# Loads of the second pass's h and of wo's pages moved from SyncE's queue to ScalarE's

## The chip, the cores and the metric

The kernel runs on one core of one Trainium2 chip. A core has TensorE (PE, with its weight loads shown as PEld), VectorE (DVE), ScalarE (ACT), GpSimd (POOL) and SyncE (SP), each with its own stream of instructions that it works through in order, and they meet through semaphores. SyncE computes nothing here: its stream holds the DMAs that it issues. The time is device microseconds of one execution; for the kernel before, the median of three runs is 2241.88 us (2241.23 to 2243.62).

## The reference

One transformer block with adaptive layer norm, for one sequence of 2048 tokens by 1024 channels, 32 heads of 32 channels, all in float32:

```python
mod = (silu(c) @ w_mod)            # sa, ca, ga, sb, cb, gb
h = layernorm(x) * (1 + ca) + sa
x = x + ga * A(h)                  # attention
h = layernorm(x) * (1 + cb) + sb
x = x + gb * B(h)                  # token-mixing MLP, 2048 -> 3584 -> 2048 over tokens
# A: q, k, v = h @ wq, h @ wk, h @ wv; the tokens fall into 4 segments s of 512
logits = q_s k_s^T * scale + mask        # -1e9 where key index < query index
a_dot = softmax(logits) @ v_s
a_mem = phi(q_s) M / (phi(q_s) z + 1e-6) # phi(t) = t + 1 for t > 0, else exp(t)
o = sigmoid(beta) * a_mem + (1 - sigmoid(beta)) * a_dot
M, z = M + phi(k_s)^T v_s, z + sum(phi(k_s))   # then o @ wo at the end
```

## The kernel before, in words

**Precision.** Large products run on pairs of reduced-precision parts: an operand is held as a rounded part and the rest, and a product is three matmuls (high by high, high by low, low by high). `split` (L119) makes the two parts, the first on ScalarE, the second on VectorE.

**Attention.** The heads are in eight groups of four (`NG`), the tokens in four segments. One iteration t works on one group and one segment. The 32 iterations are ordered in two passes, `its` (L322): pass one goes through the groups with segments 0 and 1, pass two through the groups again with segments 2 and 3. The normed, transposed input h of a segment is eight pages of 128 x 2 x 512 (one for every 128 channels), in `hpages`. The pool of pages has 16 buffers, which is two segments; so pass two's sixteen pages take over the buffers of pass one's. h of segments 2 and 3 is computed during pass one by `token_tile` (L230) and parked in device memory in `hT1`; `reload_h` (L317) fetches one page, 512 KB. At the end of pass two the same 16 buffers are taken over by the pages of wo, `wop`, which were prepared in `wos` by `wo_split` (L597); a page again is 512 KB.

An iteration has these steps. `project` (L338) multiplies the pages by the group's weights: `nps` (L196) gives k and v, `qps` (L204) gives q. ScalarE and VectorE copy the results out of PSUM; the split q and k are `sg`. `stack` (L328) copies `sg` within the chip by DMA into the layout `sk` (three DMAs for a head, L334 to L336). `maxima` (L431) multiplies q and k (tiles `sx`, `sy`, `sz`, L441), takes maxima on VectorE (L443) and sends them, transposed and negated (`nt`, L451), as two more rows into `sk` by four small DMAs for two heads (L456). `scores` (L470) then multiplies again with these rows (`a`, L477 to L484), and ScalarE takes the exponentials (L478, L481, L485), which leave the two PSUM buffers of the tag `s2` that three products of a head go through in turn. `values` (L494) multiplies by v (`pv`, L506), and the group's output goes out as `ot` to `oT` (L524).

**What sets the order.** The main loop (L632) runs over head steps n, four to an iteration, and in each emits scores of n, maxima of n + 3, values of n - 1 and the projection of n + 8. Weights of the next group are fetched ahead (`load_w`, `wv` and `wq` from `wsp`, L171), rows of w_mod during these steps (`rawm`, L531). Where the code emits an instruction does not fix its place: the program is built with

```python
with tile.TileContext(nc, schedule_with_timeline_sim=True) as tc, ExitStack() as ctx:
```

so a planner lays out each engine's stream when the program is built, by the work that it reckons ready and by the code's order among that. In the kernel before all DMAs are issued by SyncE.

**Around the change.** The loads of h's pages are emitted at steps m = n + 8 = 59 to 66, two to a step, the first eight for segment 2 and the others for segment 3. They need the buffer of the old page free, so they wait for the last `qps` product of pass one that reads it: iteration 14 for the first eight, iteration 15 for the rest. The loads of wo's pages are emitted at steps 123 to 130, again two to a step, sixteen pages of which thirteen are loaded here (the other three in `product`, L727, after the loads of x). They wait likewise for `qps` of iterations 30 and 31. After the attention, `product` (L715) multiplies the output by wo (`po`, L734), the second norm is taken, and the token MLP runs as matrix products with seven multiplications in place of eight (`mix`, L849) until the end.

Of the kernel before, what the change touches and what calls it, by code (L numbers as in the profile page):

```python
# [7 lines left out]
F32 = mybir.dt.float32  # L8
# [37 lines left out]
def attention_and_mlp(ctx, tc, x, wq, wkv, wo, beta, w1, b1, w2, b2, c, wm_a, wm_b, out):  # L46
    nc = tc.nc
    V, A, G, T, SY = nc.vector, nc.scalar, nc.gpsimd, nc.tensor, nc.sync
# [9 lines left out]
    wos = dram.tile([NK, 2, P, 2, 512], F32, name="wos")  # L58
    wsp = dram.tile([NG, 6, P, 2, 512], F32, name="wsp")
    hT1 = dram.tile([2, NK, P, 2, L], F32, name="hT1")  # L60
# [84 lines left out]
    def new_page(name):  # L145
        return page.tile([P, 2, 512], F32R, tag="page", bufs=16, name=name)
# [32 lines left out]
    def load_w(g, pr):  # L179
        res = W[pr, g] = {}  # L180
        for kind, part in (("v", 0), ("v", 1), ("q", 0)):
            load_part(g, pr, kind, part, res)
        if pr == 0:
            keep_w(g)
# [93 lines left out]
    for ct in range(NK):  # L278
        for part in range(2):
# [4 lines left out]
            elif ct >= NSC:  # L284
                for i in range(2):
                    c = slice(512 * i, 512 * i + 512)
# [29 lines left out]

    def reload_h(seg, ct):  # L317
        pg = new_page(f"h{seg}_{ct}")
        SY.dma_start(pg.bitcast(F32), hT1[seg - 2, ct])
        hpages[seg, ct] = pg  # L320

    its = [(pr, g, 2 * pr + i) for pr in range(2) for g in range(NG) for i in range(2)]  # L322
# [138 lines left out]
    @contextmanager  # L461
    def behind(n, engines):

        with ExitStack() as s:
            for e in engines:
                if (n, e) in marks:
                    s.enter_context(tc.issue_after(marks[n, e].ins))
            yield
# [86 lines left out]
    def at(f, n):  # L555
        if 0 <= n < 4 * NI:
            f(n // 4, n % 4)
# [31 lines left out]
    wop = {}  # L589
# [42 lines left out]
    for n in range(-LEADS, 4 * NI + VL):  # L632
        at(scores, n)
        at(maxima, n + LEADS)
        at(values, n - VL)
        m = n + LEADP
        if 0 <= m + 4 < 4 * NI:
            t = (m + 4) // 4
            if its[t][:2] not in W:
                with tc.issue_after(last_sk[0, 3].ins):  # L640
                    load_w(its[t][1], its[t][0])
        if m >= 8:
            at(project, m)
        if 59 <= m < 67:
            seg, ct = 2 + (m - 59) // 4, 2 * ((m - 59) % 4)
            reload_h(seg, ct)
            reload_h(seg, ct + 1)
        if 4 * NI - 5 <= m < 4 * NI + 3:
            i = m - 4 * NI + 5
            for c in (2 * (i % 4), 2 * (i % 4) + 1):  # L650
                wop[c, i // 4] = new_page(f"wo{c}_{i // 4}")
                if c < 5 or i < 4:
                    SY.dma_start(wop[c, i // 4].bitcast(F32), wos[c, i // 4])
        for f, engines in todo.pop(n, ()):
            with behind(n, engines):
                f()
# [428 lines left out]
```

## Time and profile before

| what | value |
|---|---|
| median of three runs | 2241.88 us |
| the profiled execution's own time | 2241.52 us |
| its span, first to last instruction | 2239.8 us |
| mean granted TensorE clock | 0.995 |
| DVE busy | 1672.5 us (75%) |
| ACT busy | 1147.5 us (51%) |
| POOL busy | 748.9 us (33%) |
| loads of h's pages | 469.4 to 508.3 us (issue) |
| loads of wo's pages at L653 | 934.6 to 967.9 us (issue) |

The execution that was profiled took 1.7 us more than its span, and 0.36 us less than the median. Times inside the profile are microseconds from the span's start. "PE sx L441 <- DMA sk<-nt: 5.7, 1, 5.7" in the view of waits reads: TensorE, before instructions of line 441 that write tile sx, stood idle 5.7 us in all, once, at most 5.7 us, and what ended it was the landing of a DMA from nt into sk. SPq is SyncE's stream; a DMA's row there is its issue, not its transfer. A row of a timeline is: start, duration, engine, line, operation, tiles (out<-in), how many were merged, and in brackets the idle time ahead of it with what ended it. Rows of stretches give the busy time of PE, PEld, DVE, ACT and POOL, then the granted clock, the share that the 16 DMA engines were busy, and GB/s.

### The profile page before, as it was taken

How to read it: one execution, taken by the hardware profiler on the slowest of the kernel's cores; microseconds unless marked ns; L12 is line 12 of the kernel's file. 1: busy time of each engine (PE TensorE's matmuls, PEld its weight loads, DVE VectorE, ACT ScalarE, POOL GpSimd, SP SyncE). 2: the span in 40 equal slices, each digit the busy share in tenths (PEclk: the TensorE clock that was granted, in tenths of full speed). 3: DMA queues.
4: the chain of work that ended last, by engine and by line, in shares of the span. 5: the costliest groups of instructions: out<-in, count | busy, mean ns of one | idle time of the engine just before them, and what ended most of it. 6: DMA issues, size and time to landing. Idle time of an engine off the chain costs nothing.

```text
span 2239.8 us, 38394 instructions
## 1 busy us (share of the span) xinstructions
PE 2192.1 (98%) x13802; PEld 1897.4 (85%) x13802; DVE 1672.5 (75%) x3778; ACT 1147.5 (51%) x2106; POOL 748.9 (33%) x847
## 2 busy tenths in 40 slices
PE   7999999998999999999999999999999999999999
PEld 6889898888989999988888888888888888888887
DVE  6687677866777777655758866888888897868687
ACT  6487777765656666655546633533334242424232
POOL 5175666655767767654001200033330000000000
PEclk9999999999999999999999999999999999999999
DMA  6657565687557666674664687755556541414134
GB/s 264 205 168 205 155 189 163 185 299 237 148 177 217 171 199 188 202 211 145 226 216 146 228 322 265 261 193 230 205 202 237 199 152 57 156 57 146 57 122 151
DMA packets 175186, 423.06 MB, mean 189 GB/s; under 512 B 17524, under 2 KB 71828, under 8 KB 166036
## 3 DMA queue, kind: packets, MB, share of 16 engines
q1 hardware_dynamic: 174996, 420.61, 57.4%
q8 instruction: 110, 1.80, 0.3%
q14 instruction: 80, 0.66, 0.1%
HBM read 244.62 MB, written 125.06 MB: 165 GB/s over the span
## 4 chain that ended last, share of the span: by engine, by line
PE 86%; DVE 4%; DMA 4%; ACT 3%; POOL 2%; issue 1%; SPq 0%; ACTq 0%; DVEq 0%; POOLq 0%
PE mx L864 48%; PE nps L196 12%; PE qps L204 7%; PE po L734 6%; PE pv L506 3%; PE sz L441 1%; PE a L477 1%; PE sx L441 1%; POOL ph L492 1%; PE up L423 1%; PE rd L413 1%; DVE wv L126 1%; PE a L480 1%; PE sy L441 1%; PE a L484 1%
## 5 line engine op out<-in xcount | busy, mean ns | idle before, releaser
L864 PE MATMUL mx<-bU,sp 128*128 128x512 f32 x2352 | 534.1, 389 | 0.9 <-DVE ac L871 0.9
L864 PEld LDWEIGHTS mx<-bU,sp 128*128 128x128 f32 x2352 | 441.2, 188 | 93.3 <-issue 1.3
L196 PE MATMUL nps<-wv,h 128*128 128x256 f32 x3072 | 438.1, 283 | 3.2 <-POOL h L126 3.2
L123 ACT CAST sp<-wr 128x384 fp32r<-128x384 f32 (+2 forms) x408 | 217.1, 545 | 421.9 <-PE mx L864 350.2
L864 PE MATMUL mx<-bA,sp 128*128 128x512 f32 x1764 | 430.5, 389 | 0.0
L492 POOL TENSOR_TENSOR ph<-p,ph 128x640 f16<-128x640 f32 x256 | 377.9, 1498 | 147.4 <-ACT ph L490 147.0
L196 PEld LDWEIGHTS nps<-wv,h 128*128 128x128 f32 x3072 | 406.1, 190 | 10.1 <-POOL h L126 4.2
L864 PEld LDWEIGHTS mx<-bA,sp 128*128 128x128 f32 x1764 | 331.1, 188 | 68.8
L126 DVE TENSOR_TENSOR sp<-wr,sp 128x384 fp32r<-128x384 f32 (+2 forms) x408 | 260.2, 648 | 29.3 <-ACT sp L123 28.9
L871 DVE TENSOR_TENSOR ac<-mx,ac 128x512 f32<-128x512 f32 x280 | 189.3, 684 | 84.8 <-PE mx L864 84.2
L204 PE MATMUL qps<-h,wq 128*128 128x512 f32 x768 | 199.0, 402 | 0.1
L490 ACT CAST ph<-p 128x1280 f16<-128x1280 f32 x128 | 161.0, 1259 | 47.2 <-POOL p L488 46.5
L734 PE MATMUL po<-wo,ots 128*128 128x512 f32 x768 | 179.3, 390 | 0.0
L734 PEld LDWEIGHTS po<-wo,ots 128*128 128x128 f32 x768 | 143.5, 188 | 29.1
L488 POOL TENSOR_SCALAR_AFFINE_SELECT p<-p 128x256 f32<-128x256 f32 x256 | 130.4, 518 | 109.4 <-ACT p L485 59.2
L204 PEld LDWEIGHTS qps<-h,wq 128*128 128x128 f32 x768 | 142.5, 192 | 28.1 <-ACT vp L364 0.4
L864 PE MATMUL mx<-bB,sp 128*128 128x512 f32 x588 | 164.0, 389 | 0.0
L506 PE MATMUL pv<-vp,ph 128*128 128x97 bf16 (+1 forms) x2560 | 143.9, 202 | 1.8 <-POOL ph L492 1.6
L443 DVE CUSTOM_DVE_ANT_0 sx<-sx,mask 128x128 f32<-128x128 f32 (+1 forms) x256 | 94.0, 367 | 60.3 <-PE sx L441 58.6
L506 PEld LDWEIGHTS <-ph 128*128 128x128 f16 x2560 | 115.1, 98 | 24.2 <-issue 8.8
L864 PEld LDWEIGHTS mx<-bB,sp 128*128 128x128 f32 x588 | 110.4, 188 | 22.9
L871 DVE TENSOR_TENSOR cc<-mx,cc 128x512 f32<-128x512 f32 x140 | 94.7, 683 | 37.0 <-PE mx L864 36.9
(200 smaller groups left out, 3188.3 us busy)
## 6 DMA issues: line engine op xcount, KB each, us to landing
sk<-sg SPq DMA_DIRECT2D x384, 128.0 KB
wr<-in_w_dram SPq DMA_DIRECT2D x28, 1024.0 KB
wr<-in_w_dram SPq DMA_DIRECT2D x32, 768.0 KB
bstu<-ucd SPq DMA_DIRECT2D x28, 768.0 KB
wsp<-wv SPq DMA_DIRECT2D x32, 512.0 KB
rawm<-in_wm_b_dram SPq DMA_DIRECT2D x32, 512.0 KB
wv<-wsp SPq DMA_DIRECT2D x32, 512.0 KB
pcd<-cc SPq DMA_DIRECT2D x14, 1024.0 KB
```

The costliest lines, as they stand in the source:

```text
L123: last_hi[0] = A.copy(hi, src)
L126: lo_eng.tensor_tensor(lo, src, hi.bitcast(F32), op=ALU.subtract)
L196: T.matmul(ps[:, aa], h[:, j, 128 * tt:128 * tt + 128], wt[:, i, o:o + 256], start=(n == 0), stop=(n >= 6 * NK - 2), skip_group_check=True)
L204: T.matmul(ps, wt[:, i, o:o + 128], h[:, j], start=(k + n == 0), stop=(3 * k + n == 3 * NK - 1))
L443: marks[4 * t + h - LEADS, "V"] = V.tensor_tensor_reduce(o, o, mask[:, 384 - 128 * i:], 1.0, -3.0e38, op0=ALU.add, op1=ALU.max, accum_out= ...
L488: G.affine_select(w, w, pattern=[[0, 2], [1, 128]], compare_op=ALU.is_ge, fill=0.0, base=0, channel_multiplier=-1)
L490: marks[n, "A"] = A.copy(ph[:, 0], p32)
L492: marks[n, "G"] = G.tensor_tensor(ph[:, 1, c], p32[:, c], ph[:, 0, c], op=ALU.subtract)
L506: T.matmul(pv[:, i, 0:w], ph[:, part, o:o + 128], d["vp"][:, j, h, 0:w], start=(n == 0), stop=(n == 19), skip_group_check=True)
L734: T.matmul(ps, os_[:, i, P * ct:P * ct + P], wop[ct, nh][:, j], start=(n == 0), stop=(n == 3 * NK - 1))
L864: T.matmul(ps, ops[q][:, i, P * k:P * k + P], b[:, j], start=(m == 0 and first), stop=(m == 3 * nk - 1), skip_group_check=True)
L871: V.tensor_tensor(d, ps, d, op=ALU.add)
```

## The change

Two lines change the engine on whose stream the loads are issued: sixteen of h (L319) and thirteen of wo (L653). Sources, destinations, sizes and the places in the code stay; the three loads of wo at L727 and all other DMAs stay with SyncE.

```diff
     def reload_h(seg, ct):
         pg = new_page(f"h{seg}_{ct}")
-        SY.dma_start(pg.bitcast(F32), hT1[seg - 2, ct])
+        A.dma_start(pg.bitcast(F32), hT1[seg - 2, ct])
         hpages[seg, ct] = pg
...
             for c in (2 * (i % 4), 2 * (i % 4) + 1):
                 wop[c, i // 4] = new_page(f"wo{c}_{i // 4}")
                 if c < 5 or i < 4:
-                    SY.dma_start(wop[c, i // 4].bitcast(F32), wos[c, i // 4])
+                    A.dma_start(wop[c, i // 4].bitcast(F32), wos[c, i // 4])
```

## Prediction

> **What bounds the kernel now.** I read the page first, then the waits of TensorE around the two places where the moved loads run, then stretches of 20 us, and last SyncE's stream row by row.
>
> ```profile
> span 2239.8 us, 38394 instructions
> PE 2192.1 (98%) x13802; PEld 1897.4 (85%) x13802; DVE 1672.5 (75%) x3778; ACT 1147.5 (51%) x2106; POOL 748.9 (33%) x847
> ...
> q1 hardware_dynamic: 174996, 420.61, 57.4%
> ```
>
> TensorE is busy nearly throughout, so a change to queues can win only from its holes. One queue (q1) carries all the program's DMAs. The holes near the loads, first between 455 and 530 us, then between 900 and 1020:
>
> ```profile
> PE sx L441 <- DMA sk<-nt: 5.7, 1, 5.7
> PE sz L441 <- DVE mx L443: 1.7, 1, 1.7
> PE sx L441 <- DMA sk<-sg: 1.0, 1, 1.0
> ...
> PE a L477 <- DMA sk<-nt: 1.3, 1, 1.3
> PE sx L441 <- DMA sk<-sg: 0.9, 1, 0.9
> ```
>
> ```profile
> 460.00:480.00 20.00, 18.33 (x131) 15.23 (x130) 13.28 (x29) 12.87 (x23) 13.36 (x14) 0.83 0.93 360
> 500.00:520.00 20.00, 18.52 (x187) 17.81 (x185) 14.90 (x47) 12.42 (x20) 14.92 (x16) 1.00 1.01 360
> 520.00:540.00 20.00, 15.77 (x95) 14.15 (x96) 9.69 (x32) 7.13 (x15) 5.33 (x9) 0.83 0.58 140
> ...
> 940.00:960.00 20.00, 17.82 (x165) 16.83 (x164) 12.42 (x44) 10.03 (x19) 9.51 (x14) 1.00 0.79 248
> ...
> 530.00:930.00 400.00, 394.35 (x3574) 364.21 (x3572) 289.78 (x879) 260.04 (x461) 279.27 (x334) 1.00 0.62 182
> ```
>
> Three things are to be seen. The one large hole, 5.7 us, ends at the landing of the small DMAs of nt. Both stretches with a hole around 465 and around 520 show a granted clock of 0.83, which is 0.17 x 20 = 3.4 us of full clock lost each; the 2.2 us in two pieces in 940:960 cost no clock. And in 500:520 the DMA engines are saturated (1.01, 360 GB/s). Why nt is late stands in SyncE's stream and in the chain that ended last:
>
> ```profile
> 499.05 2.52 SPq L319 DMA_DIRECT2D h<-hT  x4
> ...
> 504.12 4.53 SPq L319 DMA_DIRECT2D h<-hT  x4
> 506.91 0.32 SPq L319 DMA_DIRECT2D h<-hT  x1
> 509.56 0.32 SPq L171 DMA_DIRECT2D wv<-wsp  x1
> 510.89 0.69 SPq L334 DMA_DIRECT2D sk<-sg  x1
> 512.17 0.64 SPq L335 DMA_DIRECT2D sk<-sg  x1
> ...
> 517.23 0.62 SPq L336 DMA_DIRECT2D sk<-sg  x1
> 519.58 0.34 SPq L531 DMA_DIRECT2D rawm<-in_wm_b_dram  x1
> 522.27 2.74 SPq L456 DMA_DIRECT2D sk<-nt  x4
> ```
>
> ```profile
> 499.54 10.01 DMA h<-hT
> 509.56 12.64 DMA wv<-wsp
> ...
> 523.03 1.08 DMA sk<-nt
> ```
>
> From 504 on SyncE issues one DMA about every 1.3 us. The load of wv issued at 509.56 lands at 509.56 + 12.64 = 522.20, and nt's first DMA goes out at 522.27, the eighth issue after it (six of sk, one of rawm, then nt). So at most eight DMAs are under way, and each new one waits for the landing of the one eight before. Eight transfers of 512 KB at 360 GB/s need 11.7 us, which is about that 12.64: the hole is made by the queue of h's pages ahead of nt.
>
> **The change part by part.** It removes 29 issues from SyncE's stream (16 of h, 13 of wo) and adds them to ScalarE's. No byte and no transfer goes away.
>
> ```profile
> L319 SPq EVENT_SEMAPHORE  x16: 17/17/17, 469.3 to 508.3; - x16
> L319 SPq DMA_DIRECT2D h<-hT x16: 319/320/1062, 469.4 to 508.3; - x16
> ...
> L653 SPq DMA_DIRECT2D wo<-wos x13: 320/439/858, 934.6 to 967.9; - x13
> ...
> SPq L319 <- PE qps L204: 2.8, 6, 0.9
> SPq L319 <- DMA wq<-wsp: 2.7, 2, 1.9
> SPq L653 <- PE qps L204: 3.0, 5, 1.4
> ```
>
> *Issue time on ScalarE.* 16 x 0.320 + 13 x 0.439 = 10.8 us, if an issue there costs what it costs on SyncE; no row shows one on ScalarE. Bounds: 0 (all under ScalarE's idle time) and 10.8. ScalarE is busy 12.9 and 12.4 us of 20 in the rows 460 and 500, so most of it has cover. Two ScalarE rows bear on that:
>
> ```profile
> 474.29 0.58 ACT L481 ACTIVATE p<-a,shift 128x384 f32<-128x384 f32 x1 [2.98 <-PE a L480]
> ...
> 936.62 1.14 ACT L123 CAST ots<-otr 128x512 fp32r<-128x512 f32 x2 [2.63 <-DMA otr<-oT]
> ```
>
> The first eight loads of h wait for the same `qps` products for which ScalarE idles anyway until 474.29: 8 x 0.32 = 2.6 under 2.98 of idle, nothing on the path; were that idle gone, 2.6. The first eight of wo fall beside 936.62 and later, where ScalarE then works without a pause: 8 x 0.439 = 3.5 us on the path. The five last loads of wo (2.2 us) find ScalarE with slack and cost nothing; without it 2.2. So +3.5.
>
> The Trainium skill, "DMA: Bandwidth & Descriptors", section "Issuing engines are not separate DMA queues", says that all issuers' DMAs run on the same 16 engines and that more issuers save only the time to initiate. By that rule the transfers would stay as they are, and this +3.5 would be the whole change, 2245.4; by the rows further down it is not, because what is moved is waits too.
>
> *The waits that go with it.* This is the larger part. A load waits for its buffer and for the landing of the DMA eight before, and now all of ScalarE's later work stands behind that: copies of sg, exponentials, nt.
>
> ```profile
> 501.03 0.58 ACT L123 CAST sg<-qps 128x512 fp32r<-128x512 f32 x1
> 502.19 0.58 ACT L481 ACTIVATE p<-a,shift 128x384 f32<-128x384 f32 x1 [0.58 <-PE a L480]
> ...
> 501.81 0.34 PE L480 MATMUL a<-sk 98*128 98x384 f32 x1
> ...
> 504.46 0.39 PE L477 MATMUL a<-sk 98*128 98x512 f32 x1
> ```
>
> The buffers of segment 3 come free one by one while `qps` of iteration 15 runs, so a planner that goes by readiness puts the first seven loads ahead of the copy of sg, which needs the whole product. On SyncE the last four waited for landings, and the seventh went out at 506.91. If ScalarE has to stand there too, the copy starts at 507.2 in place of 501.03, and L481 ends at 507.2 + 0.6 + 0.6 = 508.4 in place of 502.8. The product at 504.46 takes the same PSUM buffer as the one at 501.81 (two buffers, three products), so it needs L481 done: TensorE stands from 504.5 to 508.4, 3.9 us. Bounds: 0, if the loads land early enough or are planned behind the exponentials (the slack is 504.46 - 502.8 = 1.7 us), and 3.9. I take 3.9, since the limit of eight and the full DMA engines stay. What is late next is the hole at 518.5: TensorE arrives there 3.9 us later, while nt still waits for the transfers, so the hole shrinks from 5.7 to 1.8. Together these two give 0. But a hole of 3.9 us is larger than the one of 1.7 us that goes with the 0.83 at 460, so I count a further stretch at the lowered clock, +3.4 (bounds 0 and 6.8, none or two more), and leave the old one at 520, since 1.8 us is no smaller than that 1.7.
>
> *SyncE's side.* What comes after the loads in its stream (sk<-sg, nt, rawm, wv) no longer stands behind their waits for TensorE. At wo that can close the two holes of 1.3 and 0.9: -2.2. Bounds: -2.2 and 0; I take -2.2, because both holes end at landings of the small DMAs that stand behind these loads, and the waits of 3.0 us for TensorE in the last row of L653 are more than the two holes.
>
> *The order of the streams.* Moving 29 issues makes the planner's reckoning another one, so the order of all streams after 469 us may change; that it goes by readiness shows here, where an output that the code emits ahead of at least the last six of these eight loads went out between the seventh and the eighth:
>
> ```profile
> 469.36 5.48 SPq L319 DMA_DIRECT2D h<-hT  x7
> 476.11 0.32 SPq L524 DMA_DIRECT2D oT<-ot  x1
> 476.75 0.32 SPq L319 DMA_DIRECT2D h<-hT  x1
> ```
>
> Between 530 and 930 TensorE idles only 400 - 394.35 = 5.65 us at full clock, so there another order can win at most 5.65 and can add a hole with its clock, 5.7 + 3.4 = 9.1. I take one hole of the small kind, +1.7.
>
> **Sum.** Issues +3.5, holes 0, clock +3.4, SyncE's side -2.2, order +1.7: +6.4 us. Against the profiled execution's 2241.52 that is 2247.9; the median lies 0.36 higher, so 2248.
>
> **The rivals.** *Faster: SyncE's small transfers pass the pages.* With two queues, wv at 509.56 has not seven pages ahead but shares the engines with them: at the 1.28 us between SyncE's issues at 510.89 and 512.17, it lands after two such steps, near 512, and nt goes out before TensorE needs it at 518.5. Then 5.7 + 3.4 + 2.2 = 11.3 us go, less 3.5 of issues: 2241.9 - 7.8 = 2234. With the hold of 3.9 on ScalarE it is 2238. For it: nt itself takes 1.08 us once issued. Against it: the limit of eight seems to be one for all DMAs, and 500:520 is full of bytes that all still have to move. It decides for this rival if ScalarE's hold stays under the slack of 1.7 us. The Trainium skill, "DMA: Bandwidth & Descriptors", section "Queues, rings and completion order", says that a DMA engine goes round the queue rows that have work, packet by packet; by that rule the small transfers do pass the pages, as this rival has it, and the trace of before cannot show it, with q1 alone.
>
> *No change: the hole only moves.* ScalarE holds TensorE 3.9 us at 504, the hole at 518 shrinks by as much, one lowered clock replaces the other, and the order does no harm: +3.5 - 2.2 = +1.3, 2243. For it: the saturated 500:520. Against it: it needs three things to balance.
>
> *Clearly slower: ScalarE's waits spread.* If all 10.8 us of issues and the waits of 2.8 + 2.7 + 3.0 us reach TensorE, with a lowered clock more than in the sum, it is 10.8 + 8.5 + 3.4 - 2.2 = +20.5: 2262. For it: 530:930 has almost no hole to swallow anything. Against it: ScalarE idles a third of the time there.
>
> **How the numbers follow.** The forecast (2246 to 2256) has 0.40, clearly slower 0.12, no change 0.18, faster 0.30. 0.2% is 4.5 us, about what a measurement of this kernel can tell from no change. So faster 0.30, same 0.18, slower 0.52. The range goes down to 2233, which leaves out some 0.08 where the faster case wins all 11.3 us, and up to 2262, which leaves out about 0.07. The likeliest case's own range is 2246 to 2256.
>
> **What would show it.** A second queue with 29 x 512 KB = 15.2 MB in the list of queues; rows of L319 on ScalarE's stream ending in waits for landings around 500 to 508; the copy of sg after them; TensorE waiting for ScalarE (L478 or L481) near 505; the wait for nt at 518 smaller; the clock at 0.83 in one stretch more. The prediction is wrong if ScalarE's loads go out without waits over 1.7 us, or if the wait for nt is gone and no other is in its place.

## The result, and the profile after

The changed kernel took 2252.82 us (median of six runs, 2251.45 to 2257.52) against 2241.06 us for the kernel before beside it (2237.68 to 2243.62): a ratio of 1.0059, interval [1.0049, 1.007], so it is slower by more than the 0.2% that a measurement tells apart. The profiled execution took 2251.55 us with a span of 2249.8 us, 10.0 us more than the span before. These 10.0 us are what has to be found; the medians lie 11.8 us apart, so the two profiles show most of the difference and not all of it.

The page of the kernel after, its first lines and its list of queues:

```profile
span 2249.8 us, 38379 instructions
PE 2194.4 (98%) x13802; PEld 1898.2 (84%) x13802; DVE 1679.3 (75%) x3778; ACT 1145.5 (51%) x2106; POOL 751.1 (33%) x847
...
q1 hardware_dynamic: 170820, 405.40, 55.3%
q10 hardware_dynamic: 4176, 15.21, 1.9%
```

The second queue is there, with the 15.2 MB of 29 pages. The span less TensorE's busy time is 55.4 us, against 2239.8 - 2192.1 = 47.7 before: TensorE stands 7.7 us longer. Its busy time itself, for the same 13802 matmuls, is 2.3 us longer; the stretches below show that TensorE worked longer at a lowered clock. 7.7 + 2.3 = 10.0. The waits of TensorE from 420 to 1060 us, and below them the waits of ScalarE from 455 to 530:

```profile
PE a L480 <- ACT p L485: 11.7, 1, 11.7
PE a L477 <- DMA sk<-nt: 4.0, 1, 4.0
PE sz L441 <- DVE mx L443: 2.9, 2, 1.7
```

```profile
ACT p L485 <- DMA oT<-ot: 14.0, 1, 14.0
```

The old hole of 5.7 us before sx is gone. In its place TensorE stands 11.7 us, once, for an exponential of ScalarE, and ScalarE stood 14.0 us ahead of that exponential (L485) until a DMA landed. ScalarE's own stream from 498 to 516 us, with its DMA issues (ACTq):

```profile
498.74 0.33 ACTq L319 DMA_DIRECT2D h<-hT  x1
...
503.86 0.33 ACTq L319 DMA_DIRECT2D h<-hT  x1
509.26 0.33 ACTq L319 DMA_DIRECT2D h<-hT  x1
511.94 0.33 ACTq L319 DMA_DIRECT2D h<-hT  x1
513.59 0.33 ACTq L319 DMA_DIRECT2D h<-hT  x1
513.96 0.58 ACT L485 ACTIVATE p<-a,shift 128x384 f32<-128x384 f32 x1 [14.04 <-DMA oT<-ot]
...
515.01 0.58 ACT L123 CAST sg<-qps 128x512 fp32r<-128x512 f32 x1
```

Seven of segment 3's eight loads stand ahead of L485, the last four of these seven (503.86 to 513.59) wait for landings, and the copy of sg starts at 515.01 in place of 501.03. The last of the landings waited for is that of oT, in the chain that ended last:

```profile
500.90 12.61 DMA oT<-ot
```

500.90 + 12.61 = 513.51, and the next load goes out at 513.59. So SyncE's DMA, 256 KB, holds a load that ScalarE issues. The reason stands in the operands that the trace keeps: all DMAs of SyncE and ScalarE signal their landings on the same eight semaphores, and each waits, before it goes out, until the DMA that used its semaphore last has landed. oT at 500.90 and the load at 513.59 both use semaphore 101. So the limit of eight is one that this program sets itself, for both engines together; that the chip has such a limit is not shown. Why the landings come so late is in the list of queues from 495 to 520 us (packets, MB, share of the 16 engines), after and then before:

```profile
q1 hardware_dynamic: 1333, 3.98, 46.1%
q10 hardware_dynamic: 1127, 4.13, 44.1%
```

```profile
q1 hardware_dynamic: 2383, 7.94, 89.2%
```

The same 8 MB at the same total share; but the engines now divide their time between the two queues. SyncE's oT stood behind four pages of weights issued from 498.96 on and landed 12.6 us after its issue, and from 509.26 to 511.94 ScalarE's loads are 2.7 us apart, where SyncE issued one about every 1.3 us before. The Trainium skill, "DMA: Bandwidth & Descriptors", section "Queues, rings and completion order", has the engines go round the queues that hold work; the two shares agree with that, but not with what the faster rival in the prediction made of it, that SyncE's transfers would therefore land earlier.

The second place is at wo. SyncE's stream from 938 to 964 us after, and from 936 to 950 before:

```profile
942.47 0.36 SPq L718 DMA_DIRECT2D otr<-oT  x1
946.09 0.69 SPq L334 DMA_DIRECT2D sk<-sg  x1
957.24 0.65 SPq L335 DMA_DIRECT2D sk<-sg  x1
957.99 2.63 SPq L456 DMA_DIRECT2D sk<-nt  x4
```

```profile
938.59 0.37 SPq L718 DMA_DIRECT2D otr<-oT  x1
939.05 4.18 SPq L653 DMA_DIRECT2D wo<-wos  x6
943.32 0.68 SPq L334 DMA_DIRECT2D sk<-sg  x1
945.13 0.65 SPq L335 DMA_DIRECT2D sk<-sg  x1
946.42 3.46 SPq L456 DMA_DIRECT2D sk<-nt  x3
```

Before, a load of otr (the attention's output coming back for the product with wo, a page of 512 KB) went out at 938.59 and let the waiting L335 go at 945.13, at most 6.5 us later, with six pages of wo behind it in the same queue. After, it went out at 942.47 and let L335 go at 957.24, 14.8 us later. (L335 uses the semaphore of this load in both kernels, so it goes out when the load has landed.) Eight pages of wo are on the other queue at that time. SyncE's waits from 940 to 985 us say the same:

```profile
SPq L335 <- DMA otr<-oT: 10.4, 1, 10.4
```

Behind that wait stand the small DMAs of nt; TensorE waits 4.0 us for them. How the engines shared their time meanwhile is in the list of queues from 946 to 954 us after (packets, MB, share):

```profile
q10 hardware_dynamic: 721, 2.62, 85.1%
q1 hardware_dynamic: 697, 0.36, 15.4%
```

The engines took nearly as many packets from one queue as from the other. But the packets of a page of wo hold 4096 bytes and those of otr 512, because otr is read in rows of 128 floats (L718), so otr moved 0.36 MB beside the pages' 2.62. Sharing by packets holds back the transfer with the small ones. The first packets of otr came late as well: from 943 to 946 us only the pages of wo moved. Why is not shown.

Last, stretches cut at the ends of the holes, after and before (PE busy is the third number, the granted clock the third from the end):

```profile
502.90:514.60 11.70, 0.02 (x2) 0.01 (x1) 0.00 (x0) 0.64 (x2) 0.00 (x0) 0.65 1.02 390
514.60:520.10 5.50, 5.50 (x24) 5.31 (x24) 3.76 (x9) 5.15 (x9) 3.67 (x3) 0.50 1.03 381
...
960.50:967.90 7.40, 6.42 (x30) 6.06 (x30) 1.33 (x6) 1.16 (x2) 0.41 (x1) 0.55 0.75 159
...
540.00:940.00 400.00, 396.72 (x3607) 366.31 (x3606) 295.14 (x884) 258.43 (x462) 284.41 (x337) 1.00 0.63 182
```

```profile
524.20:529.60 5.40, 5.37 (x36) 4.93 (x36) 2.32 (x10) 0.65 (x2) 0.58 (x2) 0.50 0.65 149
...
540.00:940.00 400.00, 394.35 (x3586) 363.81 (x3585) 289.76 (x877) 260.53 (x462) 280.76 (x336) 1.00 0.63 184
```

The clock is halved within or just behind each large hole. That costs only where TensorE works: 5.50 x 0.50 = 2.8 us after the new hole, 5.37 x 0.50 = 2.7 us after the old one, and 6.42 x 0.45 = 2.9 us at wo, where there was none before (the clock was 1.00 in 940:960 and in 960:980). With that the 10.0 us come out as follows.

| place | holes, us | lowered clock, us |
|---|---|---|
| 500 to 530: hole of 11.7 for one of 5.7 | +6.0 | +0.1 |
| 540 to 940: idle 3.3 for 5.65 | -2.4 | 0 |
| wo, 940 to 985: 4.0 + 0.95 for 1.3 + 0.9 | +2.8 | +2.9 |
| sum | +6.4 | +3.0 |

That is 9.4 of 10.0. The start of the same instruction, after less before, says nearly the same: about +6 at 570 us, about +4.5 at 941, +10.0 at 961, and then constant to the end. So two places make it, and the second of them stood in the prediction with the opposite sign.

### The profile page after: what moved, and what is told of

Same layout as the page of the kernel before. It is cut to its first block, busy times and chain, and to the rows that moved or that the text cites. A ratio compares the mean times of both kernels' runs of the same rounds, so it can differ in the third digit from the quotient of the medians.

```text
span 2249.8 us, 38379 instructions
## 1 busy us (share of the span) xinstructions
PE 2194.4 (98%) x13802; PEld 1898.2 (84%) x13802; DVE 1679.3 (75%) x3778; ACT 1145.5 (51%) x2106; POOL 751.1 (33%) x847
## 4 chain that ended last, share of the span: by engine, by line
PE 84%; POOL 4%; ACT 4%; DMA 4%; DVE 3%; issue 1%; SPq 1%; ACTq 0%; DVEq 0%; POOLq 0%
PE mx L864 47%; PE nps L196 11%; PE qps L204 7%; PE po L734 6%; PE pv L506 3%; POOL ph L492 2%; PE a L477 1%; PE sz L441 1%; ACT ph L490 1%; PE sx L441 1%; PE a L480 1%; PE sy L441 1%; PE rd L413 1%; PE up L423 1%; DVE wv L126 1%
## 5 line engine op out<-in xcount | busy, mean ns | idle before, releaser
L871 DVE TENSOR_TENSOR ac<-mx,ac 128x512 f32<-128x512 f32 x280 | 189.3, 684 | 85.1 <-PE mx L864 84.6
```

Of the source, the lines that this page charges most:

```text
L871: V.tensor_tensor(d, ps, d, op=ALU.add)
```

## The experiments

Each kernel is the kernel before or the kernel after with the edit shown; times stand to runs of the kernel before on the same chip. One execution of each was profiled, and it can lie some us off the median of its runs: 2245.83 for 2241.39 (the first eight loads of h alone), 2245.11 for 2238.31 (the first four of segment 3), 2245.96 for 2249.05 (the last four held back). So the views tell where time goes, and the medians how much.

**The two moves by themselves.** Only the loads of h on ScalarE:

```diff
     def reload_h(seg, ct):
-        SY.dma_start(pg.bitcast(F32), hT1[seg - 2, ct])
+        A.dma_start(pg.bitcast(F32), hT1[seg - 2, ct])
```

> Only the sixteen loads of h's pages are issued by ScalarE, those of wo's pages stay with SyncE. Theory (ScalarE's stream is held by loads of h that wait for landings): the wait of TensorE for L485 near 515 us is there again with 10 to 13 us, two stretches of 6.8 us at the lowered clock around it instead of one, and the old wait for nt at 518 (5.7 us) is absent; at 940 to 960 us everything as before (waits of about 2 us, no lowered clock). Time: before plus 4 to 6 us (the +9.4 at 538 us less what the changed order gave back by 930). Rival (the new order of the streams alone costs): the wait for L485 is not needed for the loss, and about 10 us remain at the end.

Measured: 2243.32 us against 2240.76, ratio 1.0013 [1.0001, 1.0025]. The waits of TensorE from 455 to 560 and of ScalarE from 455 to 530 us:

```profile
PE a L480 <- ACT p L485: 11.7, 1, 11.7
```

```profile
ACT p L485 <- DMA oT<-ot: 14.0, 1, 14.0
```

The hold is the same to the tenth, so it belongs to the loads of h alone. The same instruction is later by about 5 us at 570 and by about 4 at 941. Then, unlike in the kernel after, the two holes at wo close (TensorE is busy 19.88 of 20 us in 940:960, 17.82 before), and 1.8 us are left in the span. That is why the total is under what was expected though the hold is as expected.

Only the loads of wo:

```diff
                 if c < 5 or i < 4:
-                    SY.dma_start(wop[c, i // 4].bitcast(F32), wos[c, i // 4])
+                    A.dma_start(wop[c, i // 4].bitcast(F32), wos[c, i // 4])
```

> Only the thirteen loads of wo's pages are issued by ScalarE. Theory (the loads of wo, all issued within some 5 us on a second queue, slow the load of otr on SyncE's, for whose landing a copy into sk waits): first part as before (wait for nt 5.7 us), near 960 us a wait for nt of 3 to 5 us and one stretch at the lowered clock: before plus 4 to 7 us. Rival (order alone): no long wait for otr's landing in SyncE's stream, and a change of less than 3 us either way.

Measured: 2248.34 us, ratio 1.0035 [1.0022, 1.0049]. SyncE's waits from 930 to 970 us, and the stretch in which its price falls:

```profile
SPq L456 <- DMA otr<-oT: 9.9, 1, 9.9
```

```profile
940.00:960.00 20.00, 14.91 (x131) 13.70 (x130) 10.78 (x39) 8.20 (x14) 8.09 (x10) 0.89 0.72 236
```

The span is 5.9 us longer, all of it from 941 to the end, by the same late otr: from 942 to 948 us 564 packets of SyncE's queue moved 0.29 MB, and 563 of ScalarE's 2.05 MB. Up to 941 the loads of h cost about 4 us, and behind it those of wo 5.9, which is about the 10.0 us of both. The two whole spans give less, 1.8 + 5.9, because the holes that close at wo when h moves alone do not close when both move. By medians the parts are 2.6 + 7.6 = 10.2 of 11.8.

**Is it the issue or the wait?** Only the first eight loads of h, which wait for TensorE's `qps` and for no landing, on ScalarE:

```diff
     def reload_h(seg, ct):
-        SY.dma_start(pg.bitcast(F32), hT1[seg - 2, ct])
+        (A if seg == 2 else SY).dma_start(pg.bitcast(F32), hT1[seg - 2, ct])
```

> Only the eight loads of segment 2 are issued by ScalarE; segment 3's and wo's stay with SyncE. Theory: these eight wait for products that ScalarE waits for anyway and find their landings done, so no wait of TensorE for ScalarE over 1 us, the wait for nt near 518 us stays at 4 to 7 us: before within 3 us. Rival (ScalarE pays for each issue, or the changed order costs): 3 to 6 us slower without a hold in ScalarE's stream.

Measured: 2241.39 us, ratio 1.0004 [0.9994, 1.0013]. Issuing from ScalarE, and waiting there for a product that ScalarE's next work needs anyway, costs nothing that these runs tell (0.13% at the upper end). ScalarE's stream of the kernel after at wo shows why:

```profile
940.49 0.62 ACT L123 CAST ots<-otr 128x512 fp32r<-128x512 f32 x1 [2.10 <-DMA otr<-oT]
940.78 0.33 ACTq L653 DMA_DIRECT2D wo<-wos  x1
941.02 0.61 ACT L123 CAST ots<-otr 128x512 fp32r<-128x512 f32 x1
941.14 0.45 ACTq L653 DMA_DIRECT2D wo<-wos  x1
941.54 0.58 ACT L123 CAST sg<-kps 128x512 fp32r<-128x512 f32 x1
```

The issue runs while the instruction before it computes: casts start at 940.49, 941.02 and 941.54 with an issue between each pair.

**The hold taken away.** The kernel after, with the last four loads of segment 3 planned behind ScalarE's exponentials of head step 54 (`behind` orders what follows behind an engine's last instruction of a step):

```diff
-            reload_h(seg, ct)
-            reload_h(seg, ct + 1)
+            with behind(54 if seg == 3 and ct > 3 else -99, "A"):
+                reload_h(seg, ct)
+                reload_h(seg, ct + 1)
```

> As the changed kernel, but the last four loads of segment 3 are placed in ScalarE's stream behind the cast of step 54, some 10 us later, so that the copy of sg and the exponentials of two steps no longer stand behind them. Theory: the wait for L485 falls from 11.7 to under 2 us, with at most one stretch of lowered clock near 520; the loss at wo's pages stays (5.7 us). Time: 2240 to 2247, 6 to 12 us below the changed kernel. Rival (two queues slow each other's landings, wherever the loads stand): TensorE still loses 8 us or more between 500 and 530 us.

Measured: 2249.05 us, ratio 1.0038 [1.0024, 1.0051] to the kernel before, where the kernel after has 1.0059. TensorE's waits from 455 to 560 us:

```profile
PE a L483 <- ACT p L478: 2.5, 1, 2.5
PE a L480 <- ACT p L485: 2.4, 2, 2.1
```

The hold of 11.7 us is gone, smaller ones of 2.5 and 2.4 us stand there, and the same instruction is earlier than in the kernel before by 2.7 us at 941. The loss at wo stays: later by 3.5 us at 961, 6.2 us more than at 941. Of the 6 to 12 us that were expected below the changed kernel 3.8 came, between medians. That the hole of 11.7 us had itself replaced one of 5.7 explains a part; the rest is not traced.

The other way to take the hold away is to give ScalarE only the first four loads of segment 3 and leave all other loads with SyncE:

```diff
     def reload_h(seg, ct):
-        SY.dma_start(pg.bitcast(F32), hT1[seg - 2, ct])
+        (SY if seg == 2 or ct > 3 else A).dma_start(pg.bitcast(F32), hT1[seg - 2, ct])
```

> Of h's loads only the first four of segment 3 are issued by ScalarE; segment 2, the last four of segment 3 and wo stay with SyncE. Theory (what holds ScalarE is loads that must wait for landings, and the first four need not): no wait of TensorE for ScalarE over 2 us near 515, lowered clock in one stretch at most, and the old wait for nt near 518 to 524 back at 3 to 6 us: within 3 us of before. Rival (any load of segment 3 on ScalarE holds it): a wait of TensorE for L481 or L485 of 3 us or more.

Measured: 2238.31 us against 2239.49, ratio 0.9995 [0.9985, 1.0005]. No wait of TensorE for ScalarE over 0.6 us is left from 455 to 560 us. The old wait for nt is not back either, though it was expected; TensorE waits 3.0 us for VectorE and 2.7 us for sg there. So it is the last four loads that carry the hold, by where they stand and what they wait for.

**The loss at wo taken away.** The loads of wo on ScalarE, but the first eight each behind ScalarE's work of two steps earlier, which spreads them (h stays with SyncE):

```diff
-                    SY.dma_start(wop[c, i // 4].bitcast(F32), wos[c, i // 4])
+                    with behind(n - 2 if i < 4 else -99, "A"):
+                        A.dma_start(wop[c, i // 4].bitcast(F32), wos[c, i // 4])
```

> Only wo's loads are issued by ScalarE, as in the run with wo alone, but the first eight are spread: each pair stands in ScalarE's stream behind the cast of the head step two before, so four of the eight come some 7 to 14 us later. Theory (the crowd of pages on the second queue slows otr's load, whose landing SyncE's stream then waits for): otr's second load lands within 10 us of its issue in place of 14, SyncE's wait for it falls from 9.9 to under 5 us, TensorE's wait for nt from 4.1 to under 2.5; before plus 0 to 4 us. Rival (a second queue slows the first one's landings however few pages it carries, or wo's loads cost by their place in ScalarE's stream): still 5 us or more slower than before.

Measured: 2243.83 us against 2239.49, ratio 1.0017 [1.0007, 1.0026]: 4.3 us, where the bunched loads cost 7.6. SyncE's stream from 936 to 962 us:

```profile
938.56 0.36 SPq L719 DMA_DIRECT2D otr<-oT  x1
...
942.96 2.63 SPq L456 DMA_DIRECT2D sk<-nt  x4
```

The small DMAs of nt go out without a wait for otr, whose last packets move before 944. What is left is a hole of 2.8 us at another nt, more than expected, and the clock is 0.91 in 940:960. The 4.3 us cannot be put down to wo alone: in this run's profile the old hole near 520, where nothing was moved, is 8.3 us in place of 5.7.

**Another engine.** ScalarE's stream is one that TensorE waits for. GpSimd, busy 33%, might bear the waits better. The sixteen loads of h on GpSimd:

```diff
     def reload_h(seg, ct):
-        SY.dma_start(pg.bitcast(F32), hT1[seg - 2, ct])
+        G.dma_start(pg.bitcast(F32), hT1[seg - 2, ct])
```

> The sixteen loads of h's pages are issued by GpSimd in place of ScalarE; wo's stay with SyncE. Theory (an engine that computes must not carry loads that wait): ScalarE is free of the 14 us hold, but GpSimd's work (masks L488, casts' rests L492) stands behind the loads' waits for their buffers, so TensorE waits for GpSimd's ph by 2 to 6 us in 460 to 530; time from before to before plus 8 us. Rival (it is only ScalarE's stream that matters): no new wait over 1.5 us, and the wait for nt gone, 4 to 9 us faster than before.

Measured: 2237.0 us against 2239.49, ratio 0.9983 [0.9974, 0.9993]. GpSimd's stream from 498 to 508 us and the stretch of the old hole:

```profile
499.80 2.14 POOL L319 DMA_DIRECT2D h<-hT  x4
501.96 2.78 POOL L492 TENSOR_TENSOR ph<-p,ph 128x640 f16<-128x640 f32 x2
504.68 1.62 POOL L319 DMA_DIRECT2D h<-hT  x3
```

```profile
520.00:540.00 20.00, 19.83 (x176) 17.31 (x175) 13.12 (x40) 12.52 (x25) 11.26 (x16) 1.00 0.58 155
```

Four loads go out in 2.14 us and three in 1.62, 0.53 us each, with no wait for a landing among them, and neither the hole of 5.7 us nor the lowered clock after it is there. What was expected of my theory fell; of the rival the sign came, but 2.5 us in place of 4 to 9. That no landing is waited for has two reasons in the trace. GpSimd's DMAs use eight semaphores of their own (111 to 118, where SyncE's use eight from 100 to 109), so they are outside the limit of the others. And none of theirs was due: the first eight loads had landed by 492.8, and the second eight go out from 499.80 on.

Both groups, and wo's pages alone, on GpSimd (the same edit, and at L653 `G.dma_start` for `SY.dma_start`):

> All 29 loads on GpSimd. Theory: GpSimd's loads wait for no landing of a DMA of SyncE (the sixteen of h alone did not), so no stream is held at 500, and the time at h stays as with h alone on GpSimd, 2237. At wo the pages still go out eight at a time ahead of the second load of otr; if it is the sharing of the DMA engines with a second queue that makes otr's landing late, the copy into sk waits for it again and 3 to 6 us come on top: 2240 to 2243. Rival: at wo too GpSimd's own work spaces the issues (half a microsecond each, and products between them), so that otr lands in time: 2234 to 2238.

> Only wo's thirteen loads on GpSimd. The same two at wo alone: theory, otr's second load lands 12 us or more after its issue and nt is late, before +3 to +6 us (2243 to 2246); rival, no late landing, within 2 us of before or faster by the two small holes of 2.2 us (2238 to 2242).

Measured: both 2240.89 us against 2241.04, ratio 0.9996 [0.9986, 1.0006]; wo alone 2241.55 us, ratio 0.9999 [0.9988, 1.0011]. With wo alone on GpSimd, SyncE's waits from 930 to 985 us and TensorE's from 920 to 1000:

```profile
SPq L334 <- DMA otr<-oT: 7.6, 1, 7.6
```

```profile
PE a L477 <- DMA sk<-nt: 1.9, 1, 1.9
```

Half of the theory holds: otr, issued at 938.21, lets SyncE go on at 953.21, 15.0 us later, so it is late with the pages on GpSimd's queue too (from 942 to 948 us 510 packets of SyncE's queue moved 0.26 MB, and 548 of GpSimd's 2.00 MB). The price does not follow: here the four DMAs of nt had gone out at 942.09, ahead of that wait, and TensorE loses 1.9 us where it lost 2.2 before. With both groups on GpSimd it is alike: SyncE waits 8.6 us for otr and TensorE 2.0 us for nt. So the time of both, which the theory had at 2240 to 2243, did not come about by its mechanism. What a late landing costs is decided by what the planner put behind the wait.

**SyncE kept, the order changed.** If the queue of pages ahead of nt makes the old hole, moving pages behind nt should close it without another engine. The kernel before, with the last four loads of segment 3 behind nt of iteration 14's heads 0 and 1, and the first weights of pass two's second group behind nt of its heads 2 and 3 (`last_nt` holds the last small DMA of each pair):

```diff
-                with tc.issue_after(last_sk[0, 3].ins):
+                with tc.issue_after((last_nt[14, 3] if its[t][:2] == (1, 1) else last_sk[0, 3]).ins):
                     load_w(its[t][1], its[t][0])
...
-            reload_h(seg, ct)
-            reload_h(seg, ct + 1)
+            with ExitStack() as late_:
+                if seg == 3 and ct > 3:
+                    late_.enter_context(tc.issue_after(last_nt[14, 1].ins))
+                reload_h(seg, ct)
+                reload_h(seg, ct + 1)
```

> The kernel before, all loads on SyncE, but the last four loads of segment 3 stand behind the nt of step 57 (iteration 14, head 1) and the first weights of pass two's second group behind the nt of step 59. Theory (the old hole of 5.7 us is nt queued behind pages that nobody needs yet): the wait for nt near 520 falls to under 1.5 us and no lowered clock around 520; before minus 6 to 10 us, about 2232. Rival (the DMA engines are full there, so the bytes only make another hole later): a new wait of TensorE for pages or weights, time within 3 us of before.

Measured: 2237.62 us against 2239.49, ratio 0.9988 [0.9978, 0.9998]. TensorE's waits from 455 to 560 us:

```profile
PE a L478 <- DMA sk<-nt: 2.5, 1, 2.5
PE sz L441 <- DVE mx L443: 2.2, 2, 1.5
PE a L478 <- ACT ph L491: 1.9, 1, 1.9
```

The one hole of 5.7 us is gone, three smaller ones have come, and the clock is 0.92, 0.91 and 0.91 in 500:520, 520:540 and 540:560. The gain is 1.9 us in place of 6 to 10. The rival is right about the time, within 3 us of before, and about other holes; but it had TensorE wait for pages or weights, and the new waits are for nt, VectorE and ScalarE. That the bytes cause them is not shown, since the edit changes the planner's order too. Of all versions only this one and h on GpSimd lie below the kernel before with their whole interval, and both gains, 0.12% and 0.17%, are under the 0.2% that the prediction takes for telling.

## Why the prediction was right or wrong

The sign came out, and the time lies inside the likeliest case's own range: 2248 forecast, 2252.82 measured. The change itself was forecast as +6.4 us and measured as +10.0 in the profile and +11.8 between medians. The terms did worse than their sum: the holes were taken at 0 and came to +6.0 at the first place, two terms had the wrong sign, one was nothing, and the clock's was at the other place. Errors of +6.0 and +5.0 us met errors of -3.5 and -4.1, so that the sum came as near as it did is in part luck.

- **The hold of ScalarE, +3.9: right in mechanism, mis-sized; it measured 11.7.** The waits that go with the loads did move to ScalarE, the copy of sg did come after them, and TensorE waited for an exponential. But the step took the landings at SyncE's old pace, so that the seventh load would go out at 506.9. On two queues that share the engines the seventh went out at 513.6, when oT had landed. The instruction held was L485, whose product was complete, and not only what follows the copy of sg; so TensorE stood from 502.9, not from 504.5.
- **The hole at 518.5, -3.9: it went wholly, -5.7.** With 11.7 us of delay ahead of it nt had landed. Together the two steps are +6.0 where the prediction had 0. That is the main error.
- **The lowered clock, +3.4 near 505 with the old one left: wrong place, near in size.** One stretch replaced the other there (2.8 for 2.7). The new one came at wo, 2.9 us. The conversion was too large as well: 0.17 x 20 = 3.4 counts the part of the lowered clock that falls into the hole, where it costs nothing; only TensorE's work at half clock counts.
- **SyncE's side, -2.2 at wo: wrong in sign; it measured +2.8 of holes and +2.9 of clock.** The step saw that nt would no longer stand behind waits for TensorE. It did not see that otr landed early while the pages of wo stood behind it in the same queue, and that from a queue of its own its small packets move about a seventh of the pages' bytes (0.36 to 2.62 MB). When wo stays with SyncE and only h moves, these two holes do close.
- **Issue time, +3.5: 0.** It added the issue to ScalarE's stream as if it could not overlap the instruction before it. The lower bound that was given was the right value, but not for the reason given with it, since between the casts at wo ScalarE had no idle time to hide it: the issues ran beside them.
- **Changed order, +1.7: -2.4.** Between 540 and 940 us TensorE stood 3.3 us in place of 5.65, which is inside the bounds that were given.
- **The rivals.** The faster one needed SyncE's transfers to pass the pages; they landed later instead (oT after 12.6 us). The case in which the hole only moves had the right picture, but the new hole is twice the old. Clearly slower, 2262, had ScalarE's issue time and its waits for `qps` in it, which the run with the first eight loads alone priced at nothing. The rule of the Trainium skill, "DMA: Bandwidth & Descriptors", section "Issuing engines are not separate DMA queues", by which more issuers save only issue time, agrees with the bytes (8 MB at 89 to 90% share in 495:520, before and after). The reading that then only issue time would change fails, because waits and the order of landings moved as well.

What is not settled: why the first packets of otr moved only near 946, 3.7 us after its issue (near 939.6, 1 us after it, in the kernel before), and how much of each run's small difference is the planner's new order.

## What to carry to other kernels

When a DMA is moved to another engine's stream, list what it will wait for there, landings of other engines' DMAs among them, and read which compute instruction stands behind it: here the issue itself cost nothing and the wait 14.0 us of ScalarE. A second queue does not bring bytes sooner when the DMA engines are full; it takes the order between queues away, so look for the transfer that was early because it stood ahead in the one queue, first of all one with small packets. And count a lowered clock only over the work that runs in it.

## What the hardware showed that was not expected

- Two busy queues shared the DMA engines by packets: 46.1% and 44.1% of the time with packets mostly of 4096 bytes in both, but 85.1% and 15.4% where one queue's packets had 4096 bytes and the other's 512 (721 and 697 packets). A 512 KB DMA of small packets took up to 14.8 us there, and at most 6.5 with all in one queue.
- An issue on ScalarE (0.326 us median for h's pages) ran beside the cast ahead of it; on GpSimd one took 0.53 us.
- After holes of 11.7 and of 4.0 us, as after the old one of 5.7, TensorE ran at half clock for 5.4 to 7 us; after the two of 1.25 and 0.95 us at wo before, the clock stayed at 1.00. The length of the hole alone does not decide it: the hole of 1.7 us near 465 us before was followed by 6 us at half clock, the one of 1.9 us at wo with wo alone on GpSimd by none (1.00 in 940:960).
